# Two softmax attentions and a squared-ReLU layer: transposes moved from VectorE and TensorE to the DMA engines

## The chip, the core and the metric

The kernel runs on one core of a Trainium2 chip. The engines are TensorE (PE in the profile, its weight loads PEld), VectorE (DVE), ScalarE (ACT), GpSimd (POOL) and SyncE (SP, which only issues DMAs). The metric is the device time of one launch in microseconds; less is better.

## What is computed

Eight batches, eight heads, a sequence of 576 rows, head size 64. 32 packed queries `p` per head first attend over the whole sequence, and then every row of the sequence attends over the 32 packed results, which serve as keys and as values. The output, with heads side by side (4608 rows of 512), goes through two layers with a squared ReLU between them.

```python
def sm_attn(qq, kk, vv):
    s = scale * np.matmul(qq, kk.transpose(0, 1, 3, 2))
    s = s - np.max(s, axis=-1, keepdims=True)
    a = np.exp(s)
    a = a / (np.sum(a, axis=-1, keepdims=True) + 1e-09)
    return np.matmul(a, vv)
p_packed = sm_attn(p, k, v)
out = sm_attn(q, p_packed, p_packed)
...
h = x @ w_in                    # 512 -> 2048
g = np.maximum(h, 0.0) ** 2
return (g @ w_out)              # 2048 -> 512, float32
```

## The kernel before

The order of all work is written out by hand, as some 1,390 words in one string, `ORDER`; each word is one step, and each engine runs its steps in the order of the words. There is no loop over batches in the program: steps of different batches are woven together, the layers of batch b between the attention of batch b + 1.

A word names a step, a batch and a quad (four heads, so that two quads make a batch): `kT30` is the turn of the keys of batch 3, quad 0. The steps of the attention, in the order of its data:

- `Lk`, `Lq`, `Lv`: loads of keys, queries and values, issued by POOL, which casts them from float32 to bfloat16 on the way (lines 233 to 242). Keys and queries come as 128 partitions (4 heads x 32 rows) by 18 x 64. Each of the three kinds has three buffers, so a load waits for the reader of the third load before it.
- `kT`, `qT` (lines 279, 285): DVE transposes keys and queries in 32 x 32 blocks of pairs of bfloat16. The result has 32 pairs of head elements on 32 partitions per head. Two buffers each.
- `s1` (line 295): scores of the packed queries. A contraction over 64 head elements is done in two passes (`e`, even and odd elements) of 32 rows, on 32x32 tiles of the PE array. From batch 2 on both quads of a batch go together, eight tiles side by side; for the second quad, `group` (line 245) moves heads to other tile positions.
- `m1` (DVE maximum, line 316), `x1` (ACT exponential with its sum, line 321), `rd` (reciprocal, line 328).
- `eT` (line 339): six PE transposes of the exponentials into PSUM; `eo` copies them to SBUF on DVE or ACT (lines 334, 332).
- `pv` (line 352): the packed result, contracted over the sequence in six chunks; `pp` scales it (lines 360, 362), `bd` is a DVE transpose of it for the second scores (line 367); `pt`, `po` are a PE transpose and its copy (lines 372, 332, 334), which `w0` and `w1` read.
- `s2` (line 295), `t2`, `m2`, `sb`, `x2`, `su`, `a2`, `aT`: scores of the sequence rows and the second softmax, mostly on DVE (lines 383 to 415).
- `w0`, `w1` (line 422): the packed results times `w_in`, on 64x32 tiles; `W0`, `W1` copy this to SBUF.

Then `h` (line 438, first layer), `r` (ReLU on ACT or DVE, lines 444, 446), `q` (square on DVE, line 479), `o` (second layer, line 490), and `c` (copy to SBUF and two stores from SP's queue, line 510).

The packed queries of batches 0 and 1 are loaded first by SP (line 170) and turned by DVE; those of batches 2 to 7 come by one POOL DMA (`Pr`, line 552), and `Pt` turns and scales them on DVE (lines 211, 217).

PSUM: the tag `a` (two buffers of two banks) is shared by all scores, transposes, `ps_pv` and `ps_wp`; `ps_h` and `ps_o` have two buffers each in the later stages. `o_sb` has three buffers.

Of the kernel before, what the change touches and what calls it, by code (L numbers as in the profile page):

```python
# [21 lines left out]
D = 64  # L22
# [9 lines left out]
PAIRED = range(2, 8)  # L32
# [9 lines left out]
Lk00 Lk01 Lq00 kT00 P0 Z32 s100 kT01 I m100 x100 Z5 s101 m101 x101 Lq01 P1 Z7 eT00 Lv00 eo00:a Lk10 Z10 pv00 rd00  # L42
qT00 rd01 qT01 pp00:v bd00 eT01 kT10 Lv01 Z3 s200 Wi00 Wi01 pt00 eo01:a Lk11 Z5 pv01 s110 pp01:a t200 pt01 Wi10 bd01
m200 sb00:p m110 s201 x110 t201 x200 m201 su00 Z10 eT10 po01:v eo10:a a200:v Z12 w001 sb01:p po00:a x201 su01 Wi11
aT00 w000 Lv11 a201:p kT11 W001:a Z11 s111 Lv10 W000:a aT01 h0.8 m111 h0.11 r0.8:a h0.9 r0.11:v h0.2 x111 r0.9:a
w101 q0.8 h0.3 r0.2:v W101:a Lq11 eT11 eo11:a rd11 h0.10 Lq10 q0.9 rd10 w100 r0.3:v W100:a h0.1 r0.10:v h0.0 q0.3
pv11 Wo0 r0.1:a q0.11 Pr r0.0:v h0.5 q0.2 pp11:a h0.6 pv10 r0.5:a qT11 r0.6:a pt11 bd11 q0.1 h0.14 pp10:a q0.10
r0.14:a h0.12 s211 h0.15 q0.0 r0.12:a h0.7 r0.15:a po11:v qT10 r0.7:a w011 Wo2 t211 Lk21 h0.13 q0.6 W011:a q0.5 h0.4
bd10 r0.4:a w111 s210 r0.13:v Wo1 o0.0 q0.7 m211 sb11:v o2.0 x211 W111:a t210 o2.1 Lk20 m210 o3.0 Wo3 o1.0 o0.1 o0.2
q0.15 o1.1 su11 o1.2 Pt pt10 po10:a q0.4 o2.2 o3.1 w010 Lv20 w110 o0.3 Lq21 o3.2 o3.3 o0.4 q0.13 o2.3 W010:a Lv21  # L50
o1.3 kT21 q0.12 W110:a kT20 a211:p o1.4 q0.14 sb10:p x210 su10 o1.5 o0.5 s12 o2.4 o2.5 a210:p m120 x120 o0.6 m121
o1.6 aT11 aT10 o0.7 c0:v o1.7 x121 o2.6 c1:a o2.7 h1.0.0 qT21 h1.0.6 eT20 eT21 rd21 r1.0.6:v rd20 r1.0.0:a o3.4
h1.0.4 Lq20 eo20:a h1.0.2 pv20 eo21:v pv21 r1.0.2:v r1.0.4:a h1.0.1 pp20:v h1.0.5 pt20 pp21:v c2:a r1.0.1:a r1.0.5:a
o3.5 po20:a bd21 h1.0.12 h1.0.3 w020 q1.0.2 o3.6 r1.0.12:a r1.0.3:a h1.0.7 h1.0.13 q1.0.0 Lk30 qT20 o3.7 W020:a bd20
o4.0 r1.0.13:a c3:a r1.0.7:v q1.0.1 h1.0.10 q1.0.6 h1.0.11 q1.0.3 s22 r1.0.10:a h1.0.8 r1.0.11:a r1.0.8:a h1.0.9
Lq30 o4.1 t220 h1.0.14 r1.0.9:a o4.2 t221 q1.0.4 r1.0.14:a h1.1.0 r1.1.0:a pt21 h1.0.15 m221 o4.3 po21:a h1.1.2
r1.0.15:a w021 w120 q1.0.5 h1.1.10 o5.0 sb21:v r1.1.2:a W021:a o4.4 h1.1.8 m220 x221 Lv31 r1.1.10:a sb20:v o5.1 Lk31
r1.1.8:a x220 o4.5 h1.1.3 r1.1.3:a h1.1.11 o4.6 r1.1.11:a kT30 W120:a h1.1.4 kT31 r1.1.4:a w121 q1.0.7 h1.1.1 o5.2
o4.7 r1.1.1:a h1.1.6 o5.3 su20 W121:a su21 Lq40 h1.1.5 r1.1.5:a r1.1.6:v c4:a o5.4 s13 a221:v h1.1.7 q1.1.0 r1.1.7:a
h1.1.14 q1.1.5 o5.5 r1.1.14:a h1.1.15 r1.1.15:a a220:v Lk40 o5.6 aT21 o5.7 q1.1.1 q1.1.2 h1.1.12 q1.1.3 Lk41 aT20  # L60
c5:a h1.1.13 Lq31 r1.1.12:a o6.0 o6.1 h1.1.9 r1.1.13:a r1.1.9:a o6.2 Lv41 m131 h2.0.2 q1.1.4 r2.0.2:a h2.0.3 o6.3
m130 h2.0.0 r2.0.3:a o6.4 h2.0.4 kT40 q1.1.7 r2.0.0:a x130 o7.0 h2.0.8 r2.0.4:a o6.5 Lv30 r2.0.8:a eT30 x131 h2.0.6
rd30 o7.1 eo30:v h2.0.7 o7.2 eT31 r2.0.6:a q1.1.6 o6.6 o6.7 qT30 r2.0.7:a rd31 qT31 q2.0.1 h2.0.1 h2.0.14 pv30
eo31:a r2.0.1:a pv31 o7.3 pp31:a c6:a r2.0.14:v h2.0.5 q2.0.0 o7.4 h2.0.10 pp30:a r2.0.5:v o7.5 bd30 r2.0.10:a
h2.0.12 pt30 r2.0.12:a o7.6 h2.0.9 h2.0.11 po30:a kT41 w030 bd31 w130 r2.0.11:a W030:a r2.0.9:v q2.0.3 h2.1.6 q2.0.2
r2.1.6:a h2.0.13 o7.7 r2.0.13:a o8.0 W130:v c7:a h2.0.15 h2.1.7 r2.0.15:a s23 q2.0.4 h2.1.0 r2.1.7:v q2.0.7 o8.1
r2.1.0:a h2.1.14 t230 o8.2 t231 h2.1.12 r2.1.14:a Lq41 q2.0.6 m231 o8.3 o8.4 Lv40 r2.1.12:a pt31 q2.0.5 h2.1.1 o8.5
o9.0 h2.1.15 r2.1.1:a h2.1.4 r2.1.4:a o8.6 r2.1.15:a o9.1 o8.7 m230 h2.1.10 po31:v sb31:v o9.2 h2.1.13 x231 o9.3
o9.4 r2.1.10:a sb30:v su31 r2.1.13:a h2.1.8 q2.1.3 c8:a w131 w031 q2.1.0 h2.1.11 o9.5 x230 r2.1.8:v r2.1.11:a a231:v
W031:a q2.1.6 h2.1.2 o9.6 r2.1.2:v h2.1.5 su30 o9.7 a230:v q2.1.7 h2.1.3 aT31 W131:a r2.1.5:a o10.0 o10.1 o10.2 s14  # L70
h2.1.9 aT30 c9:a r2.1.3:a o10.3 q2.1.1 h3.0.8 o10.4 o10.5 r2.1.9:a r3.0.8:a h3.0.2 h3.0.0 m140 q2.1.4 x140 m141
r3.0.2:a x141 q2.1.2 q2.1.5 o11.0 eT40 eo40:v h3.0.6 o11.1 r3.0.0:a rd41 o11.2 h3.0.3 eT41 r3.0.6:a h3.0.1 qT40 qT41
r3.0.3:a o10.6 Lk50 eo41:a r3.0.1:v h3.0.7 o10.7 rd40 q3.0.1 pv40 pv41 r3.0.7:a pp40:v q3.0.0 h3.0.4 h3.0.5 pt40
o11.3 r3.0.4:a h3.0.9 c10:v Lk51 o11.4 r3.0.5:v r3.0.9:a q3.0.4 o11.5 h3.0.10 o11.6 po40:a pp41:a h3.0.12 pt41 bd40
r3.0.10:a q3.0.3 h3.0.14 r3.0.14:v r3.0.12:a o11.7 h3.0.15 bd41 w140 po41:a q3.0.2 w040 r3.0.15:v h3.1.2 W040:a
o12.0 W140:a o12.1 r3.1.2:v h3.0.11 o12.2 o12.3 kT51 q3.0.7 r3.0.11:v h3.1.0 kT50 s24 h3.1.4 r3.1.0:v c11:a o12.4
t241 o12.5 r3.1.4:a o12.6 h3.1.5 o12.7 r3.1.5:a h3.0.13 q3.0.5 r3.0.13:a o13.0 h3.1.6 o13.1 m241 c12:a sb41:v h3.1.3
r3.1.6:a r3.1.3:a x241 t240 o13.2 h3.1.1 r3.1.1:a o13.3 h3.1.7 o13.4 o13.5 r3.1.7:a q3.0.6 Lv51 m240 sb40:v h3.1.8
Lq51 w141 w041 q3.1.2 o13.6 o14.0 r3.1.8:a x240 h3.1.9 su41 o13.7 o14.1 Lv50 h3.1.14 W041:a c13:a a241:v r3.1.9:v
r3.1.14:a h3.1.15 o14.2 su40 W141:a o14.3 q3.1.1 h3.1.12 o14.4 r3.1.15:a s15 aT41 h3.1.10 o14.5 Lv61 a240:v o14.6  # L80
r3.1.12:a q3.1.0 h3.1.13 r3.1.10:a aT40 q3.1.4 m150 m151 h4.0.2 r3.1.13:a o15.0 o15.1 h4.0.10 r4.0.2:a o14.7 q3.1.6
q3.1.3 o15.2 x150 h4.0.4 r4.0.10:a o15.3 h3.1.11 c14:v r4.0.4:v x151 eT50 eo50:a q3.1.7 eT51 h4.0.8 r3.1.11:v q3.1.5
o15.4 h4.0.5 Lk61 r4.0.8:v o15.5 eo51:v h4.0.12 Lk60 r4.0.5:v pv50 pv51 h4.0.9 rd51 r4.0.12:a o16.0 h4.0.11 Lq50
r4.0.9:a q4.0.4 rd50 o16.1 r4.0.11:a pp50:v pp51:a h4.0.3 o16.2 pt51 qT50 o15.6 h4.0.0 po51:v r4.0.3:a r4.0.0:a
q4.0.5 o15.7 Lq60 h4.0.14 pt50 c15:a q4.0.1 h4.0.1 o16.3 r4.0.14:a o16.4 po50:v r4.0.1:v h4.0.15 h4.1.0 w050 q4.0.2
w150 bd51 r4.1.0:a r4.0.15:a o16.5 h4.0.6 kT60 q4.0.0 h4.1.1 r4.1.1:a q4.0.7 o16.6 bd50 r4.0.6:v o17.0 h4.1.2 Lk71
W050:a h4.1.3 r4.1.2:a W150:v o17.1 o17.2 qT51 r4.1.3:a h4.0.13 kT61 r4.0.13:a h4.0.7 q4.0.6 s25 h4.1.6 t251
r4.0.7:a t250 o16.7 q4.1.0 o17.3 o17.4 o17.5 c16:a m250 r4.1.6:a h4.1.10 h4.1.4 r4.1.4:a o17.6 sb50:v w151 w051
r4.1.10:a h4.1.5 h4.1.11 o17.7 m251 o18.0 r4.1.5:a h4.1.8 r4.1.11:a o18.1 Lq71 q4.0.3 qT60 c17:a h4.1.9 Lk70 o18.2
q4.1.2 o18.3 o18.4 o18.5 r4.1.8:a sb51:v W051:a o18.6 o19.0 x250 r4.1.9:a x251 W151:a h4.1.12 h4.1.7 q4.1.1 o18.7  # L90
c18:a o19.1 r4.1.12:a Lq61 su50 s16 a250:v o19.2 su51 a251:v m160 h4.1.14 r4.1.7:a o19.3 h4.1.13 o19.4 aT50
r4.1.14:a x160 o19.5 aT51 q4.1.3 m161 Lv60 h4.1.15 o19.6 r4.1.13:a h5.0.10 o20.0 r4.1.15:a h5.0.2 x161 q4.1.5 q4.1.4
o19.7 r5.0.2:a o20.1 eT61 r5.0.10:v h5.0.6 h5.0.3 eT60 c19:v r5.0.6:a o20.2 r5.0.3:v eo60:a q4.1.6 h5.0.4 eo61:v
r5.0.4:a h5.0.7 o20.3 q5.0.1 rd61 pv60 r5.0.7:a rd60 pp60:v pv61 h5.0.0 q4.1.7 Lv70 h5.0.11 o20.4 pt60 r5.0.0:a
h5.0.1 o20.5 r5.0.11:v pp61:a h5.0.5 o21.0 r5.0.1:a o20.6 po60:a h5.0.8 r5.0.5:a h5.1.2 qT61 kT71 q5.0.5 w160 q5.0.3
bd60 w060 q5.0.2 r5.0.8:a r5.1.2:a W060:a o21.1 h5.0.9 kT70 o21.2 W160:a r5.0.9:v bd61 Lv71 o20.7 o21.3 h5.1.3
q5.0.0 r5.1.3:v h5.0.14 s26 t260 h5.0.15 c20:a r5.0.14:a h5.0.12 r5.0.15:a r5.0.12:a o21.4 h5.1.0 o21.5 r5.1.0:a
q5.1.1 t261 h5.1.12 r5.1.12:a h5.1.1 o22.0 q5.0.4 r5.1.1:a h5.0.13 m260 o22.1 r5.0.13:v o21.6 h5.1.4 pt61 r5.1.4:a
sb60:v po61:a h5.1.13 o21.7 r5.1.13:a h5.1.6 o22.2 m261 q5.0.7 h5.1.14 x260 r5.1.6:a o22.3 r5.1.14:a o22.4 c21:a
sb61:v h5.1.5 h5.1.7 r5.1.5:a r5.1.7:a o22.5 su60 w061 q5.1.6 w161 q5.0.6 h5.1.15 h5.1.8 Lq70 x261 a260:v r5.1.15:a  # L100
q5.1.0 q5.1.2 aT60 o22.6 W061:a o22.7 o23.0 h5.1.10 r5.1.10:v o23.1 o23.2 r5.1.8:a h5.1.11 o23.3 c22:a o23.4 W161:a
su61 h5.1.9 q5.1.3 s17 o23.5 r5.1.11:a o24.0 a261:v aT61 o23.6 m170 h6.0.6 m171 r5.1.9:a o24.1 h6.0.2 o23.7 x170
# [525 lines left out]
```

## Time and profile before

| | |
|---|---|
| Time, median of 2 runs | 250.86 us (250.03 and 251.68) |
| Span of the profiled execution | 248.6 us |
| Median less span | 2.3 us |
| PE, DVE, ACT, POOL busy | 95%, 78%, 59%, 18% |
| Granted clock of PE | 0.99 of full speed over the span |
| DMA by POOL (loads) | 18.55 MB, 47.1% of 16 DMA engines' span |
| DMA by SP (stores) | 9.44 MB, 15.0% |

The page gives no device time for the profiled execution apart from its span, so the difference of 2.3 us stands for what lies around the span.

How to read it: a row of the page's groups names the line, the engine, the operation and the tiles (out<-in), how often it ran, its busy time, the mean of one in ns, and the idle time of its engine just before with what ended it. Matmuls overlap, so the mean of one (379 ns for 512 columns) is longer than the pitch at which they follow each other. In the timeline, each line is a run of like instructions with its start and its length, both in microseconds. "To landing" is the time from the issue of a DMA to its last byte.

### The profile page before, as it was taken

How to read it: one execution, taken by the hardware profiler on the slowest of the kernel's cores; microseconds unless marked ns; L12 is line 12 of the kernel's file. 1: busy time of each engine (PE TensorE's matmuls, PEld its weight loads, DVE VectorE, ACT ScalarE, POOL GpSimd, SP SyncE). 2: the span in 40 equal slices, each digit the busy share in tenths (PEclk: the TensorE clock that was granted, in tenths of full speed). 3: DMA queues.
4: the chain of work that ended last, by engine and by line, in shares of the span. 5: the costliest groups of instructions: out<-in, count | busy, mean ns of one | idle time of the engine just before them, and what ended most of it. 6: DMA issues, size and time to landing. Idle time of an engine off the chain costs nothing.

```text
span 248.6 us, 6041 instructions
## 1 busy us (share of the span) xinstructions
PE 237.1 (95%) x2415; PEld 132.2 (53%) x2447; DVE 194.2 (78%) x411; ACT 145.7 (59%) x316; POOL 45.8 (18%) x75
## 2 busy tenths in 40 slices
PE   8998899998999999999999999999999999999992
PEld 5655554465556554655456555655555555555540
DVE  1888899978988899979887998898897798644710
ACT  2346784476968748755764658676957555353100
POOL 8329634350401500033000230010000000000000
PEclk9999999999999999999999999999999999999997
DMA  6999999999791992269812794252121213211323
GB/s 112 203 207 205 206 197 209 197 142 259 161 171 64 157 211 45 46 93 187 185 42 45 135 130 122 64 90 56 42 45 42 45 42 82 49 42 44 70 63 82
DMA packets 23358, 28.52 MB, mean 115 GB/s; under 512 B 4257, under 2 KB 14753, under 8 KB 23329
## 3 DMA queue, kind: packets, MB, share of 16 engines
q0 software_dynamic: 16880, 18.55, 47.1%
q1 hardware_dynamic: 6288, 9.44, 15.0%
q8 instruction: 19, 0.31, 0.5%
q10 hardware_dynamic: 160, 0.13, 0.2%
q14 instruction: 11, 0.08, 0.1%
HBM read 37.22 MB, written 9.44 MB: 188 GB/s over the span
## 4 chain that ended last, share of the span: by engine, by line
PE 81%; DMA 10%; issue 2%; DVE 2%; POOL 2%; ACT 1%; SPq 0%; ACTq 0%; POOLq 0%
PE ps_o L490 48%; PE ps_h L438 24%; DMA v_b<-in_v_dram 4%; PE ps_wp L422 3%; PE ps_s L295 3%; DMA w_in_bf<-in_moe_w_in_dram 3%; DMA out_dram<-o_sb 3%; PE ps_e1T L339 1%; PE ps_pv L352 1%; POOL k_b L242 1%; DVE mx L387 1%; POOL d L391 0%; ACT r L444 0%; POOL q_b L242 0%; PE ps_ppT L372 0%
## 5 line engine op out<-in xcount | busy, mean ns | idle before, releaser
L490 PE MATMUL ps_o<-w_out_bf,gT 128*128 128x512 bf16 x544 | 144.2, 379 | 2.0 <-issue 0.5
L444 ACT ACTIVATE r<-ps_h 128x288 bf16<-128x288 f32 (+1 forms) x181 | 73.1, 426 | 55.9 <-PE ps_h L438 47.5
L438 PE MATMUL ps_h<-a2T,wp 128*128 128x288 bf16 x512 | 91.9, 286 | 1.4 <-ACT r L444 1.4
L490 PEld LDWEIGHTS <-gT 128*128 128x128 bf16 x576 | 54.9, 98 | 42.1 <-issue 3.3
L438 PEld LDWEIGHTS <-wp 128*128 128x128 bf16 x512 | 47.4, 98 | 44.4 <-issue 7.7
L479 DVE TENSOR_TENSOR gT<-r 128x576 bf16<-128x576 bf16 x128 | 54.7, 448 | 5.2 <-ACT r L444 4.9
L446 DVE TENSOR_SCALAR r<-ps_h 128x288 bf16<-128x288 f32 (+1 forms) x59 | 28.5, 484 | 20.0 <-PE ps_h L438 18.8
L332 ACT CAST wp<-ps_wp 128x1024 bf16<-128x1024 f32 x29 | 28.9, 1016 | 3.8 <-PE ps_wp L422 3.7
L332 ACT COPY o_sb<-ps_o 128x512 f32<-128x512 f32 x27 | 15.9, 588 | 10.8 <-PE ps_o L490 9.4
L321 ACT ACTIVATE e<-ps_s,nm 128x576 bf16<-128x576 f32 x16 | 11.8, 736 | 13.0 <-DVE nm L316 13.0
L233 POOL DMA_DIRECT2D v_b<-in_v_dram x16 | 11.1, 695 | 44.2 <-PE ps_pv L352 22.5
L279 DVE STREAM_TRANSPOSE kT<-k_b 128x576 uint32<-128x576 uint32 x16 | 15.0, 943 | 5.1 <-DMA k_b<-in_k_dram 5.1
L263 PE MATMUL ps_idle<-nought 128*128 128x288 bf16 x95 | 14.4, 304 | 1.1 <-DVE nought L178 1.1
L383 DVE STREAM_TRANSPOSE s<-ps_s 128x576 f32<-128x576 f32 x16 | 12.0, 767 | 2.4 <-PE ps_s L295 2.4
L401 DVE TENSOR_REDUCE sums<-e 128x18 f32<-128x576 f32 x16 | 11.9, 741 | 1.4 <-ACT e L396 1.3
L242 POOL DMA_DIRECT2D k_b<-in_k_dram x16 | 9.0, 562 | 21.4 <-DVE kT L279 12.5
L422 PE MATMUL ps_wp<-w_in_bf,ppT 64*32 64x512 bf16 x256 | 11.4, 382 | 0.8 <-DMA w_in_bf<-in_moe_w_in_dram 0.7
L316 DVE TENSOR_REDUCE nm<-ps_s 128x1 f32<-128x576 f32 x16 | 11.6, 739 | 0.6 <-PE ps_s L295 0.6
L285 DVE STREAM_TRANSPOSE qT<-q_b 128x576 uint32<-128x576 uint32 x16 | 12.0, 761 | 0.0
L387 DVE TENSOR_REDUCE mx<-s 128x18 f32<-128x576 f32 x16 | 11.9, 743 | 0.1
L396 ACT ACTIVATE e<-d 128x576 f32<-128x576 f32 x16 | 11.0, 685 | 1.6 <-DVE d L391 1.4
L263 PEld LDWEIGHTS <-nought 128*128 128x128 bf16 x95 | 9.2, 103 | 4.9 <-issue 1.2
(47 smaller groups left out, 153.0 us busy)
## 6 DMA issues: line engine op xcount, KB each, us to landing
out_dram<-o_sb SPq DMA_DIRECT2D x70, 128.0 KB, 2.8
k_b<-in_k_dram POOLq DMA_DIRECT2D x16, 288.0 KB, 8.1
v_b<-in_v_dram POOLq DMA_DIRECT2D x16, 288.0 KB, 7.4
q_b<-in_q_dram POOLq DMA_DIRECT2D x10, 288.0 KB, 7.2
w_in_bf<-in_moe_w_in_dram POOLq DMA_DIRECT2D x4, 512.0 KB, 12.5
w_out_bf<-in_moe_w_out_dram POOLq DMA_DIRECT2D x4, 512.0 KB, 13.8
q_b<-in_q_dram POOLq DMA_DIRECT2D x12, 144.0 KB, 3.9
p_b<-in_p_dram POOLq DMA_DIRECT2D x1, 192.0 KB, 11.5
```

What stands on the lines that cost most here:

```text
L263: self.nc.tensor.matmul(ps[:, :HALF], lhsT=self.nought[:, :P], rhs=self.nought, start=True, stop=True)
L279: return self.nc.vector.transpose(t["kT"][:].rearrange("p (j l a) e -> p a j l e", j=J, a=3).bitcast(U32).rearrange("p a j l e -> p a j (l ...
L285: return self.nc.vector.transpose(t["qT"][:].rearrange("p s e -> p (s e)").bitcast(U32), t["q"][:].rearrange("p t d -> p (t d)").bitcast(U32))
L332: engine.copy(out, x)
L383: nc.vector.transpose(s2[:].rearrange("p (a t) i -> p a (t i)", a=2), t["ps_s2"][:, :, :HALF])
L387: self.nc.vector.tensor_reduce(out=t["mx"], in_=t["s2"], op=ALU.max, axis=AX.X)
L422: self.nc.tensor.matmul(ps[NP * h:NP * h + NP, c, :], lhsT=t["ppT"][D * c:D * c + D, NP * g:NP * g + NP], rhs=self.w_in_bf[D * c:D * c + D ...
L438: self.nc.tensor.matmul(ps, lhsT=t["wp"][:, fb // n, fb % n * P:(fb % n + 1) * P], rhs=t["a2T"][:, hf * HALF:(hf + 1) * HALF], start=(qd = ...
L444: engine.activation(r, ps, ACT.Relu)
L446: engine.tensor_scalar_max(r, ps, 0.0)
L479: (engine or self.nc.vector).tensor_tensor(out=out, in0=r, in1=r, op=ALU.mult)
L490: self.nc.tensor.matmul(self.o[tt], lhsT=self.gT[:, fb, a:a + P], rhs=self.w_out_bf[:, fb, :], start=(i == 0), stop=(i == self.NFB - 1))
```

## The change

From batch 2 on (`TURNED`):

- Keys and queries (`kT`, `qT`) are transposed by DMA from SP's queue, 128 x 1152 into nine blocks of 128 x 128: rows of even `t` come to partitions 0 to 63 and of odd `t` to 64 to 127, with the 64 head elements on the partitions.
- The packed queries are loaded twice, side by side (`p_d`, two POOL DMAs), scaled by DVE and turned by one DMA (`pX`).
- Scores contract over 64 rows in one pass, on 64x32 tiles (`scores2`): 16 matmuls a batch and step where there were 32. The second scores read `ppT`, the PE transpose of the packed result, and `bd` goes; `t2` undoes the new order of rows.
- The exponentials are written into one of two fixed tiles with chunks padded to 128 columns, and a DMA from SP's queue turns them (`eT`); the PE transposes and the copies `eo` go.
- `group` goes; each query load is one DMA.

The words of `ORDER` are the same 1,390. Moved are `kT` and `qT` (each to just behind its load, or behind the scores that free its buffer, so mostly earlier), and `pt` with `po` (to just behind `pp`).

```diff
@@ p_rest
-        g0, g1 = 2 * self.NQ, self.B * self.NQ
-        self.p_turn(g0, g1)
-        x = self.pT[:, g0:, :]
-        self.nc.vector.tensor_scalar_mul(x, x, SCALE)
+        self.nc.vector.tensor_scalar_mul(self.p_d, self.p_d, SCALE)
+        self.nc.sync.dma_start_transpose(self.pX, self.p_d[:].rearrange("p g e d -> p (g e d)"))
@@ new
+    def st_turned(self, t, n):
+        x = t[n + "T"] = self.tp.tile([P, 2 * S], BF16, name=n + "T")[:].rearrange("p (t l) -> p t l", l=P)
+        self.nc.sync.dma_start_transpose(x, t[n][:].rearrange("p t d -> p (t d)"))
+    def scores2(self, *quads):
+        for h in range(QH):
+            c = slice(NP * h, NP * h + NP)
+            for e in range(2):
+                r = slice(D * e, D * e + D)
+                for ps, x, y in quads:
+                    self.nc.tensor.matmul(ps[c, e, :HALF], lhsT=x[r, c], rhs=y(r, c), start=True, stop=True)
@@ st_s1
+                x.append((t["ps_s1"], self.pX[:, (b - TURNED[0]) * self.NQ + qd, :],
+                          lambda r, c, y=t["kT"]: y[r, :, c].rearrange("p (a b) l -> p b l a", a=3)))
+            return self.scores2(*x)
@@ st_s2
+                x.append((t["ps_s2"], t["ppT"], lambda r, c, y=t["qT"]: y[r, :, c]))
+            return self.scores2(*x)
@@ st_exp1
+            e1 = t["e1"] = self.e1s[(b * self.NQ + qd) % len(self.e1s)]
+            t["den"] = self.sm.tile([P, 1], F32, name="den")
+            self.nc.scalar.activation(e1[:, :, :PS].rearrange("p (a b) s -> p a b s", a=2),
+                                      t["ps_s1"][:, :, :HALF].rearrange("p a (b s) -> p a b s", b=3), ACT.Exp,
+                                      bias=t["nm"], accum_out=t["den"])
@@ st_e1T
+            t["e1T"] = self.tp.tile([P, J, P], BF16, name="e1T")
+            self.nc.sync.dma_start_transpose(t["e1T"], t["e1"][:].rearrange("p j s -> p (j s)"))
+            return
@@ step, word "Pr"
-            self.nc.gpsimd.dma_start(self.p_b[:, g0:g1, :], self.packed(g0, g1))
+            for e in range(2):
+                self.nc.gpsimd.dma_start(self.p_d[:, :, e, :], self.packed(TURNED[0] * self.NQ, self.B * self.NQ))
@@ ORDER, batch 2
-... h1.0.0 qT21 h1.0.6 eT20 eT21 rd21 ... Lq20 eo20:a h1.0.2 pv20 eo21:v pv21 ... h1.0.1 pp20:v h1.0.5 pt20 pp21:v c2:a
+... h1.0.0 h1.0.6 eT20 eT21 rd21 ... Lq20 qT20 eo20:a h1.0.2 pv20 eo21:v pv21 ... h1.0.1 pp20:v pt20 po20:a h1.0.5 pp21:v pt21 po21:a c2:a
...
```

## The prediction

> **What bounds the kernel now.** I read the page's busy shares first, then the busy time by stretches, then the timeline around the steps that change, then the landing times of the DMAs. (Columns of the stretches: length, busy us of PE, PEld, DVE, ACT and POOL with their instructions, granted clock, DMA share, GB/s.)
>
> ```profile
> span 248.6 us, 6041 instructions
> PE 237.1 (95%) x2415; PEld 132.2 (53%) x2447; DVE 194.2 (78%) x411; ACT 145.7 (59%) x316; POOL 45.8 (18%) x75
> ```
> ```profile
> 47.00:100.00 53.00, 51.56 (x593) 28.92 (x602) 45.88 (x98) 38.41 (x88) 12.55 (x21) 1.00 0.81 152
> 100.00:150.00 50.00, 49.48 (x526) 27.70 (x532) 44.26 (x95) 31.92 (x74) 8.08 (x14) 1.00 0.62 112
> 150.00:209.00 59.00, 58.42 (x602) 32.42 (x610) 50.46 (x109) 39.60 (x92) 1.23 (x2) 1.00 0.28 58
> ```
>
> From the first scores of batch 2 (46.9 us) on, PE is busy 97 to 99% of every stretch at a granted clock of 1.00. The starts of its runs follow each other at the pitch of the matmuls (216 ns for 512 columns, 123 for 288); the few larger gaps of some 220 ns fall where a 512-column record is missing. So PE has no waits to give away: work taken from PE shortens the end one for one, and each new wait of PE lengthens it one for one. DVE, at 86 to 89%, does not end PE's waits. What decides is whether a DMA put into PE's chain lands before PE gets there.
>
> **What the change takes from PE.** The timeline shows the price of each removed step, from its start to the next run's.
>
> ```profile
> 46.91 0.70 PE L295 MATMUL ps_s<-kT,pT 32*32 32x288 bf16 x32
> 47.55 0.82 PE L490 MATMUL ps_o<-w_out_bf,gT 128*128 128x512 bf16 x3
> ...
> 102.46 0.50 PE L339 MATMUL ps_e1T<-ident,e 128*96 128x128 bf16 x6
> 102.80 0.41 PE L438 MATMUL ps_h<-a2T,wp 128*128 128x288 bf16 x2
> ...
> 110.51 0.62 PE L422 MATMUL ps_wp<-w_in_bf,ppT 64*32 64x512 bf16 x16
> 111.07 0.42 PE L438 MATMUL ps_h<-a2T,wp 128*128 128x288 bf16 x2
> ```
>
> Six transposes of the first softmax cost 0.34 us of PE; 12 such groups (batches 2 to 7, two quads) go: -4.0 us. The 32 score matmuls of a batch cost 0.64 us in four rounds of eight tiles. The new 16 stand on the 64x32 tiles that ps_wp uses; its 16 take 0.56 us, two rounds of 512 columns at 0.216 and 0.125 beside them. Two rounds of 288 are then 0.125 + 2 x 0.123 = 0.37 us, 0.27 less in each of 12 score steps: -3.2. Keys are now read with a step of three blocks per column, which no row shows; if that undid the gain, it would be 0. PE: -7.2 (at least -4.0).
>
> DVE loses 12 kT (943 ns), 12 qT (761), 12 bd (195) and its copies of e1T, some 25 us, and ACT its e1T copies (794 ns each). Neither ends anything while PE is the bound: counted as nothing.
>
> **What it adds: 37 turns on SP's queue.** 24 are of 288 KB (keys, queries), 12 of 192 KB (the exponentials, two per batch) and one of 384 KB (packed queries). SP had one load and the output stores; now the stores, the turns and the waits for loads stand in one line. No turn is in this trace. The nearest rows are SP's own DMAs.
>
> ```profile
> out_dram<-o_sb SPq DMA_DIRECT2D x70, 128.0 KB, 2.8
> k_b<-in_k_dram POOLq DMA_DIRECT2D x16, 288.0 KB, 8.1
> p_f<-in_p_dram SPq DMA_DIRECT2D x1, 128.0 KB, 2.2
> ```
> Landing of the output stores issued from 50 to 56 us, while loads were in flight:
> ```profile
> DMA to landing us min/median/max: 6.9/7.3/7.6
> ```
> And of those issued after 150 us, with few loads beside them:
> ```profile
> DMA to landing us min/median/max: 2.3/2.4/3.5
> ```
>
> Even 128 KB takes 2.2 to 2.4 us with the DMAs idle and over 7 behind loads. In the packet records, p_f's 512 packets of 256 bytes took 18 ns each, 0.6 us on 16 engines, so 1.6 of its 2.2 us is fixed. A turn moves rows of 128 two-byte elements, 256 bytes. At p_f's pace the exponentials (768 rows) take 0.86 us, keys 1.3, packed queries 1.7: the lower bound. If every element went by itself, the 4-byte packets (9 ns) would give 9216 x 9 = 83 us for keys: the upper bound. The row is nearer, but a block that is crossed is no plain copy; I take twice p_f's pace: 1.7, 2.6 and 3.5 us, and 3.3 us from issue to landing of one idle turn of exponentials.
>
> [...]
>
> Now each place where PE can wait for a turn.
>
> (a) *First scores of batch 2.* The last k_b before them landed at 44.66; DVE turned it from 45.63 to 46.57, PE began at 46.91. The second copy of the packed queries delays this load by 0.6 (in the trace p_b landed 0.64 after w_out ahead of it). SP then issues kT20 (0.6 of SP per issue, as the stores) and behind it, at 45.9, the turn of the packed queries, with loads in flight until 51.4. Landing as a store there, 7.3, plus 3.0 more transfer, would be 56; since some loads drain meanwhile I take 55.1, a wait of 8.2. With p_f's pace and nothing ahead it is 2.5; behind all loads, 12.
>
> (b) *Exponentials of batch 2.* From the scores' end to pv are 5.6 us (47.61 to 53.21), less 0.7 for the transposes gone: 4.9. The second exp ends 2.4 after the scores; a turn among loads lands 7.3 + 1.2 later: 10.9. Wait 6.0 (1 to 10).
>
> (c) *Batches 3 to 7.* The timeline of batch 4 shows the slack:
> ```profile
> 101.81 0.20 ACT L321 ACTIVATION_READ_ACCUMULATOR e<-ps_s,nm 128x1 f32 x1
> ...
> 102.91 0.20 ACT L321 ACTIVATION_READ_ACCUMULATOR e<-ps_s,nm 128x1 f32 x1
> ...
> 105.93 0.56 PE L352 MATMUL ps_pv<-v_b,e1T 96*32 96x64 bf16 x48
> ```
> The second exp ends at 103.11, pv begins at 105.93: 2.8. The others: 78.08 to 80.59, 130.05 to 132.81, 157.73 to 161.22, 184.23 to 186.80; less 0.67 each the five sum to 10.8. No load was in flight there. With exps 1.1 apart the second turn lands 1.6 + 2 x 1.7 - 1.1 = 3.9 after its exp; 0.5 for issue and release makes 4.4. Waits: 5 x 4.4 - 10.8 = 11.2. At p_f's pace it is 3.0 each, 4.3 in all.
>
> (d) *The turn of the packed result* (pt) moves to just behind pv, since the new scores read ppT. Before, pp ended at 54.04 and pt began at 54.20 with four layer-1 matmuls between it and pv; now one or two (0.245) stand where pp (0.35) and two releases (0.2) must pass. 12 x 0.3 = 3.5 (1 to 5).
>
> (e) *Queues behind.* On SP the exponentials of batch 3 stand behind qT31, which waits for a load that POOL issues behind one that waits for kT30. Before, that query landed at 71.84, 4.8 us before the first exp ended; one loaded turn in that line uses this up. The late ones also bunch ACT's and DVE's work behind PE's waits. I add 4 (0 to 10). Stores are hidden by three o_sb buffers: 72 issues in 249 us; held longer than two tiles' time (7 us), the copy and PE's ps_o would wait.
>
> **Sum.** -7.2 + 8.2 + 6.0 + 11.2 + 3.5 + 4.0 = +25.7 us on the span of 248.6: 274.3. The median of the runs is 250.86, 2.3 above that span, so I forecast 277. All lower bounds: +1.6, 252.5. All upper ones, with the exponentials of rival 1: +66, 317.
>
> **Rivals.** *1: a turn holds SP or the DMAs for 4 us or more.* For it: no row shows a turn, and the bound by elements is far. Then a pair of exponentials lands 1.6 + 8 - 1.1 + 0.3 = 8.8 after the second exp: 5 x 8.8 - 10.8 = 33; (a) 12, (b) 10, (d) 3.5, and 24 keys and queries on a 96 us occupied queue cost some 15 in (e): 250.9 - 7.2 + 73.5 = 317, from there upwards. Against: p_f's 256-byte packets. [...]
>
> *2: the queues are harmless and only batch 2 waits*, all at p_f's pace: 252 to 256. Against: 7.3 us for stores among loads.
>
> *3, the other side: the turns hide.* If one landed within 1.9 us of its exp and the packed queries before 46.9, only (d) at 1 and 1 us of (a) stay: 250.9 - 7.2 + 2 = 245.7. It decides from 2 us landing; the fastest idle DMA of SP took over 2.0, and loads triple that.
>
> *4: the 64x32 tiles don't run side by side* in this order: 16 x 0.123 = 2.0 instead of 0.37, 12 x 1.6 = 19 more, 296. Against: ps_wp.
>
> **Numbers.** The forecast (258 to 300) 0.52; rival 1 to 340 0.20, beyond 0.08; rival 4 0.06; rival 2 0.09; rival 3 0.05. The range 254 to 340 leaves out some 0.18. About 2% (5 us) is what a measurement can tell. Faster comes from rival 3's lower part, 0.04; within 2% (to 255.9) from the rest of it and rival 2, 0.07; slower 0.89.
>
> **What would show it.** Right: PE near 88% with idle time before pv and the first scores of batch 2, ended by the turns' DMAs; e1T landing 3 to 5 us after issue, keys of batch 2 over 6; 16 score matmuls in 0.37 us; DVE near 170 us busy. Wrong: landings under 2.5 us (then 255), turns of 4 us on SP (then 317), or PE waits at the relu or at loads instead.

## The result and the profile after

The changed kernel took 294.01 us (median of 2 runs, 293.16 and 294.86), the kernel before 250.86. The ratio is 1.171, with a 95% interval of 1.158 to 1.184: 43 us slower. The forecast was 277 with a range of 254 to 340. Times and ratios are those of each kernel's undisturbed executions; where a profile below is of a longer one, its span is given beside it.

The page of the kernel after, with the lines that answer to those shown of before:

```profile
span 291.4 us, 5579 instructions
...
PE 245.8 (84%) x2183; PEld 128.2 (44%) x2183; DVE 173.1 (59%) x367; ACT 142.5 (49%) x311; POOL 44.4 (15%) x72
...
PEclk9999999557789899999999979999999799999999
...
PE 61%; DMA 25%; SPq 3%; DVE 3%; ACT 2%; POOL 2%; issue 1%; ACTq 0%; POOLq 0%
```

PE's share fell from 95 to 84%; its busy time rose from 237.1 to 245.8 us, though it has 232 matmul records fewer; in part that is because some ran at half the clock (19.4 us of the busy time). The chain that ended last now runs through DMAs for a quarter of its length, and the granted clock drops to half in slices 8 and 9. The same line of the kernel before:

```profile
PE 81%; DMA 10%; issue 2%; DVE 2%; POOL 2%; ACT 1%; SPq 0%; ACTq 0%; POOLq 0%
```

PE's waits after (engine, tile and line, releaser: us in total, times, longest):

```profile
PE ps_s L299 <- DMA pX<-p_d: 18.1, 1, 18.1
PE ps_pv L382 <- DMA e1T<-e1x: 13.1, 8, 3.6
PE ps_s L299 <- DMA kT<-k_b: 4.3, 1, 4.3
PE ps_h L472 <- ACT r L478: 1.6, 5, 0.4
```

35.5 us of waits end with one of SP's turns, half of them in one place. By stretches (columns: length, busy time of PE, PEld, DVE, ACT and POOL with their instructions, granted clock, DMA share, GB/s):

```profile
47.00:100.00 53.00, 26.02 (x232) 12.21 (x232) 17.82 (x38) 17.13 (x38) 7.75 (x13) 0.77 0.96 156
100.00:150.00 50.00, 48.38 (x451) 25.23 (x437) 32.58 (x71) 30.41 (x73) 6.50 (x11) 0.97 0.88 152
150.00:209.00 59.00, 53.25 (x486) 27.09 (x485) 38.16 (x84) 33.97 (x79) 4.69 (x8) 0.97 0.80 142
```

In 53 us around batch 2's first scores PE worked 26, where it had worked 51.6. The timeline of the three longest waits, each in the brackets at the end of its line:

```profile
65.16 0.80 PE L299 MATMUL ps_s<-kT,pX 64*32 64x288 bf16 x16 [18.05 <-DMA pX<-p_d]
...
76.14 0.51 PE L382 MATMUL ps_pv<-v_b,e1T 96*32 96x64 bf16 x24 [3.56 <-DMA e1T<-e1x]
...
99.66 0.79 PE L299 MATMUL ps_s<-kT,pX 64*32 64x288 bf16 x15 [4.27 <-DMA kT<-k_b]
```

What the turns share the DMA engines with, in 14 us of the first wait, 47 to 61 (queue: packets, MB, share of 16 engines; q0 has POOL's loads, q1 SP's turns):

```profile
q0 software_dynamic: 1850, 2.26, 93.4%
q1 hardware_dynamic: 1863, 0.47, 26.5%
```

Both queues moved nearly the same number of packets (1850 and 1863; from 46 to 51 us, 784 and 785), but a load's packet has 1.2 KB on average and a turn's 256 bytes: SP's queue got 0.47 of 2.73 MB. This is where the theory for the experiments comes from: from the equal counts I estimate that the two queues take turns, one packet of each at a time. A packet of this trace is mostly one piece of 256 to 2304 bytes.

### The profile page after: what moved, and what is told of

It reads as the page before. It is cut to its first block, busy times and chain, and to the rows that moved or that the text cites. A ratio compares the mean times of both kernels' runs of the same rounds, so it can differ in the third digit from the quotient of the medians.

```text
span 291.4 us, 5579 instructions
## 1 busy us (share of the span) xinstructions
PE 245.8 (84%) x2183; PEld 128.2 (44%) x2183; DVE 173.1 (59%) x367; ACT 142.5 (49%) x311; POOL 44.4 (15%) x72
## 4 chain that ended last, share of the span: by engine, by line
PE 61%; DMA 25%; SPq 3%; DVE 3%; ACT 2%; POOL 2%; issue 1%; ACTq 0%; POOLq 0%
PE ps_o L524 37%; PE ps_h L472 18%; DMA e1T<-e1x 6%; DMA k_b<-in_k_dram 5%; DMA pX<-p_d 5%; DMA kT<-k_b 4%; DMA v_b<-in_v_dram 3%; DMA q_b<-in_q_dram 3%; PE ps_s L299 2%; PE ps_wp L456 2%; SPq L268 2%; PE ps_pv L382 1%; ACT r L478 1%; SPq L364 1%; SPq L544 1%
## 5 line engine op out<-in xcount | busy, mean ns | idle before, releaser
L524 PE MATMUL ps_o<-w_out_bf,gT 128*128 128x512 bf16 x576 | 154.6, 389 | 0.1
L472 PE MATMUL ps_h<-a2T,wp 128*128 128x288 bf16 x512 | 94.6, 293 | 1.6 <-ACT r L478 1.6
L524 PEld LDWEIGHTS <-gT 128*128 128x128 bf16 x576 | 56.3, 100 | 46.2 <-issue 6.7
L472 PEld LDWEIGHTS <-wp 128*128 128x128 bf16 x512 | 48.6, 100 | 49.0 <-issue 13.2
L513 DVE TENSOR_TENSOR gT<-r 128x576 bf16<-128x576 bf16 x128 | 55.9, 461 | 22.2 <-ACT r L478 22.0
L299 PE MATMUL ps_s<-kT,pX 64*32 64x288 bf16 x96 | 5.2, 450 | 22.3 <-DMA pX<-p_d 18.1
L340 ACT ACTIVATE e1x<-ps_s,nm 128x576 bf16<-128x576 f32 x12 | 8.8, 736 | 22.5 <-DVE nm L334 22.5
L382 PE MATMUL ps_pv<-v_b,e1T 96*32 96x64 bf16 x384 | 6.1, 201 | 13.2 <-DMA e1T<-e1x 13.1
L435 DVE TENSOR_REDUCE sums<-e 128x18 f32<-128x576 f32 x16 | 11.9, 745 | 2.6 <-ACT e L430 2.4
L240 POOL DMA_DIRECT2D q_b<-in_q_dram x16 | 8.8, 548 | 28.7 <-DMA qT<-q_b 15.7
L299 PEld LDWEIGHTS <-pX 64*32 64x32 bf16 x96 | 1.1, 93 | 25.1 <-DMA pX<-p_d 18.5
L421 DVE TENSOR_REDUCE mx<-s 128x18 f32<-128x576 f32 x16 | 11.9, 744 | 0.1
```

The lines of the kernel that those rows point to most:

```text
L240: self.nc.gpsimd.dma_start(x, s)
L299: self.nc.tensor.matmul(ps[c, e, :HALF], lhsT=x[r, c], rhs=y(r, c), start=True, stop=True)
L421: self.nc.vector.tensor_reduce(out=t["mx"], in_=t["s2"], op=ALU.max, axis=AX.X)
L435: nc.vector.reduce_sum(out=sums, in_=t["e2"], axis=AX.X)
L472: self.nc.tensor.matmul(ps, lhsT=t["wp"][:, fb // n, fb % n * P:(fb % n + 1) * P], rhs=t["a2T"][:, hf * HALF:(hf + 1) * HALF], start=(qd = ...
L513: (engine or self.nc.vector).tensor_tensor(out=out, in0=r, in1=r, op=ALU.mult)
```

## The experiments

**Theory:** a turn of 288 KB is 72 short packets on each DMA engine, and each lets one long packet of the loads by; beside loads it lands after 10 us and more. **Rivals:** the transposing itself or its issue is slow; the turns clog SP's queue for what stands behind them; the clock, lost in the waits, is what costs.

### The turn by itself

```diff
+ y = tile([P, 9, P]);      sync.dma_start_transpose(y, src)          # turn
+ y = tile([P, 9, P + 2]);  sync.dma_start(y[:, :, :P], src)          # pieces of 256 bytes
+ y = tile([P, 9, P]);      sync.dma_start(y, src)                    # whole, 2304 bytes
```

> Not the layers at all: the output is only filled with zeros; SyncE's DMAs are measured one by one. Three kinds of 288 KB moves from SBUF to SBUF: the transposing DMA, a plain copy in 256-byte pieces, a plain copy in 2304-byte pieces; first each alone, twice, then each issued behind the first landing of 14 key loads (2304-byte packets) on GpSimd's queue, and the transposing one beside 14 value loads (768-byte packets). Alone: about 3.3 us to landing for the transposing one, 2.5 to 3.5 for the copies. Theory (queues alternate packet by packet on each DMA engine, so 72 short packets per engine wait for 72 long ones): beside key loads the transposing DMA and the 256-byte copy both take 12 to 17 us, the 2304-byte copy (8 packets per engine) 4 to 7; beside value loads the transposing one 6 to 9. Rival (the transposing itself is slowed, by its unit or its issue): the 256-byte copy lands as the 2304-byte one, in 4 to 7, and the transposing one alone takes 12 or more. Rival (moves share the engines by bytes): all three copies 4 to 7.

Landing times from issue, in one execution, each of these measured once: first the turn alone; then beside key loads the turn, the copy in 256-byte pieces and the copy in whole rows; last the turn beside value loads.

```profile
DMA to landing us min/median/max: 3.2/3.2/3.2
...
DMA to landing us min/median/max: 18.1/18.1/18.1
...
DMA to landing us min/median/max: 18.4/18.4/18.4
...
DMA to landing us min/median/max: 7.6/7.6/7.6
...
DMA to landing us min/median/max: 12.1/12.1/12.1
```

Alone, the copies landed in 3.0 to 3.1 and 2.4 us. Beside the same loads the plain copy in 256-byte pieces is as late as the turn, and the same bytes in 2304-byte rows land in less than half the time. So it is the size of the packets, not the transposing; the theory holds, though all four landings lie 0.6 to 3.1 us above its numbers. The packet records show what it left out: beside loads the first packet moved 4.1 to 4.5 us after the issue, against 1.2 to 1.3 alone, and no run shows why. From the first packet to the last it then took 13.3, 13.6, 2.5 and 7.1 us. For the first two, 72 load packets of 192 ns are 13.8 us; for the last, 72 of 78 ns are 5.6. The transposing DMA was about as fast as the copy in equal pieces, alone (3.2 us against 3.0 to 3.1) and beside loads (18.1 against 18.4), and slower than the copy in whole rows (2.4 and 7.6).

### The exponentials back on TensorE

```diff
- if b in TURNED: ... self.nc.sync.dma_start_transpose(t["e1T"], ...); return
+ for j in range(J): self.nc.tensor.transpose(ps[:, j, :], t["e1"][:, j, :PS], self.ident)
```

> The changed kernel, but the exponentials of batches 2 to 7 are transposed by TensorE again (six transposes and a copy), so that only keys, queries and packed queries are turned by DMA. Theory (turns land late because their 256-byte packets alternate with the loads' long packets, and PE then waits and loses half its clock): the waits of pv for e1T, 4.6 us in batch 2 and 8.9 in batches 3 to 7, and the half clock behind them (some 3) go, 12 x 0.34 = 4.0 us of PE comes back: 294 - 13.5 - 3 + 4 = 281 us (277 to 285). The 18.2 us wait for pX and that for kT of batch 3 stay. Rival (the turns clog SP's queue, so that the ones behind are late): with 12 turns fewer ahead of them kT of batch 3 lands earlier too and its 4.6 us go as well: below 276. Rival (PE's waits are only renamed, the loads end last): 290 or more.

282.5 us, ratio 1.124 (1.117 to 1.131); the theory said 281. The waits for e1T are gone. That for pX stays (19.9), and so does that for kT of batch 3 (5.6 for 4.3), although the turns of exponentials ahead of it on SP are gone: they were not what made it late.

### Batch 2 back on VectorE and TensorE

```diff
- TURNED = range(2, 8)
+ PAIRED = range(2, 3)
+ TURNED = range(3, 8)          # kT2x qT2x pt2x po2x at their old words, heads of batch 2 paired as before
```

> Batch 2 goes back to VectorE and TensorE (keys, queries, packed queries, exponentials; steps at their old places, both quads side by side), batches 3 to 7 stay turned by DMA. Theory: the 18.2 us wait for pX, the 4.6 us for e1T of batch 2 and the half clock behind both (some 5) go, 0.8 us of PE work comes back: 294 - 28 + 1 = 267 us (263 to 271). pX itself still lands 10 us or more after its issue, but nobody waits. Rival (the loads that the turns hold back are what is late, whoever reads first): the wait comes back at the first scores of batch 3 with 8 us or more, 275 to 285.

277.4 us, ratio 1.101 (1.095 to 1.107): 10 us above the theory, inside the rival's range, but for another reason. The first wait did go; others grew. pX, which nobody waits for now, still landed 14.2 us after its issue. The stores issued from 51.57 us stood behind it in SP's queue and landed after 9.7 to 10.5 us, where such stores took 6.9 to 7.6 in the kernel before. This came through to PE:

```profile
62.84 0.59 ACT L370 COPY o_sb<-ps_o 128x512 f32<-128x512 f32 x1 [3.85 <-DMA out_dram<-o_sb]
...
63.79 0.71 PE L485 MATMUL ps_h<-a2T,wp 128*128 128x288 bf16 x4 [3.26 <-ACT r L491]
```

ScalarE's copy waits for one of three o_sb buffers to be stored, the ReLU stands behind the copy, and PE's `h` behind the ReLU: 3.3 us. Beside it come 1.5 us more of waits for e1T in batches 3 to 7 (4.0 in batch 5, whose turn landed in 4.8 us beside a load), 0.7 for kT of batch 5, and some 6.0 us lost to half clock where I had left 2.6: 8.9 of the 10.4. My reading, which no run tests by itself, is that without the long wait ahead of them batches 3 to 7 meet their loads at other places.

### The keys read as they lie

```diff
- lambda r, c: y[r, :, c].rearrange("p (a b) l -> p b l a", a=3)
+ lambda r, c: y[r, :, c]
...
- t["ps_s1"][:, :, :HALF].rearrange("p a (b s) -> p a b s", b=3)
+ t["ps_s1"][:, :, :HALF].rearrange("p e (a b l) -> p e b l a", a=3, b=3)   # the exponential's input
```

> The turned keys are read by the score matmuls in the order in which they lie (32 neighbours at a time instead of single columns 768 bytes apart); the exponential puts the columns in order as it reads PSUM. Theory (the column step halves the rate of the moving operand): the score matmul falls from 450 to about 290 ns, the step of 16 from 0.72 to 0.39 us; 6 x 0.33 = 2.0 us less if PE isn't waiting there, so 292 (291 to 294). Rival (two 64-row tiles with different lhsT cost this): no change, 450 ns stays. The exponential may take longer than 736 ns; at up to 900 this costs under 1 us.

292.4 us from two executions, ratio 1.163 (1.154 to 1.172), against 1.158 to 1.184 for the changed kernel: where the theory has it, but inconclusive in time. The groups show the mechanism. First the changed kernel's two kinds of score matmul, then this one's first kind (profile of a 295.2 us span); the mean of one is behind the bar:

```profile
L299 PE MATMUL ps_s<-kT,pX 64*32 64x288 bf16 x96 | 5.2, 450 | 22.3 <-DMA pX<-p_d 18.1 <-DMA kT<-k_b 4.3
L299 PE MATMUL ps_s<-qT,ppT 64*32 64x288 bf16 x96 | 2.8, 288 | 0.0
```
```profile
L299 PE MATMUL ps_s<-kT,pX 64*32 64x288 bf16 x96 | 3.3, 312 | 22.2 <-DMA pX<-p_d 18.1 <-DMA kT<-k_b 4.1
```

In the timeline of batch 5 the step of 16 goes from 0.72 us (157.65 to 158.37) to 0.40 (158.28 to 158.68). The exponential takes 738 ns where it took 736. So the columns 768 bytes apart cost 0.32 us a step; the time of the whole is ended by DMAs, and it doesn't show there. Why that step slows the matmul, no run shows.

### TensorE kept awake in its waits

```diff
+ def fill(self, n):      # words F140 ahead of s12, F28 pv20, F36 s13, F13 pv50, F21 pv60, F18 pv71
+     ps = self.turn32("ps_fill")
+     for _ in range(n): self.nc.tensor.matmul(ps[:, 0, :HALF], lhsT=self.nought[:, :P], rhs=self.nought, ...)
```

> The changed kernel with TensorE kept busy where it waited: 140 matmuls on zeros ahead of the first scores of batch 2, 28 ahead of pv20, 36 ahead of the first scores of batch 3, 13, 21 and 18 ahead of pv50, pv60 and pv71, some 0.123 us each, into a PSUM tile that nobody reads. The waits stay as long as before. Theory (each idle time of 2.8 us or more is followed by a stretch at half the clock, 7.6 us lost in all): the granted clock stays at 1.00 through those places and the time falls by 5 to 7.6 us, to 287 to 290. Rival (the clock falls for another reason, such as load on the chip): the half-clock stretches stay and the time is 294 to 297.

296.2 us, ratio 1.175 (1.167 to 1.184): no gain, though the clock did what the theory says, but for one stretch of 3.4 us:

```profile
PEclk9999999997999999999999999999999999999999
```

pX landed 4.5 us later in this execution, which could have hidden a gain. So once more without the 140:

> As the kernel with matmuls on zeros in TensorE's waits, but without the 140 ahead of batch 2's first scores; the 28, 36, 13, 21 and 18 ahead of pv20, batch 3's first scores, pv50, pv60 and pv71 stay. In the run with all of them pX landed 4.5 us later than in the changed kernel, which hid what the clock gave. Theory (half clock behind the later waits costs 5 us or so that nothing else covers): 294 - 3 to 5 = 289 to 291. Rival (a faster TensorE only reaches the next late DMA earlier, so that its waits grow by what the clock gives): 293 to 296, with longer waits for e1T and kT than 4.6, 4.6, 2.8, 2.8 and 2.4 us, the filled part counted in.

298.4 us, ratio 1.182 (1.176 to 1.187): no gain either, and above both ranges. Its profile (a 304.7 us span, so the waits of one long execution) has the rival's picture: the five filled waits, with 0.1225 us for each matmul of the fill, were 4.4, 6.3, 3.6, 4.3 and 3.6 us, against 4.6, 4.6, 2.8, 2.8 and 2.4. But there too pX was late, by 6.2 us, with no fill ahead of it: its landing took 13.9 us in the changed kernel, and 13.9, 15.4, 17.6 and 18.8 in the four others that issue the same work up to it. And the clock was only partly kept: it stood at half for 30.7 us, in which PE was busy for 12.3, against 34.1 and 19.4 in the changed kernel; 23.9 of them began in the first wait, which had no fill. That the clock falls to half behind long waits is shown: in the changed kernel behind five of the six places where PE waited 2.4 us or more, and with all of them filled for 3.4 us alone. Whether this costs anything of its own stays open, and so does what the fill does to the DMAs.

### The exponentials alone

```diff
+ TURNED = range(3, 8)          # into the kernel before: st_exp1, st_e1T, eo and pv of the change, nothing else
```

> The kernel before with one part of the change alone: the exponentials of batches 3 to 7 are turned by DMA, at the unchanged places in the order; keys, queries and batch 2 stay on VectorE. SP's queue carries only these ten turns and the stores. Theory (an idle turn lands 2.8 us after its issue, the second one 1.24 later at the earliest, against 2.1 to 2.8 us of slack): TensorE gives up 5 x 0.67 = 3.4 us and waits 0.6 to 1.6 us per batch, 3 to 8 in all, with half-clock stretches only behind the longest: 252.5 us (249.5 to 256). Rival (the turns behind other turns on SP made the waits): waits under 2 us in all, 249 or less.

265.3 us, ratio 1.053 (1.046 to 1.059): some 13 us above the theory and 9 above its range, and the rival fell further. In its profile (a 265.1 us span) the waits for e1T are 11.9 us where I had at most 8, and some 4.4 us were lost at half clock, 1.7 of them behind a wait for the ReLU at 60.8 us; the longest, 4.7, is for the second turn of batch 3, which was issued at 81.18, as a query load was at 81.14, and landed after 6.7 us. The other nine landed in 2.7 to 3.2 us and still made 1.0 to 2.5 us of waits in each of batches 4 to 7: an idle turn alone is too slow for this slack.

### The same with pv later

```diff
- x140 ... x141 ... eT40 ... eT41 ... pv40 pv41 ...
+ x140 eT40 ... x141 eT41 ... (some 2 us of h and o) ... pv40 ... pv41
```

> As the one above, but each turn is issued right behind its exponential and pv of batches 3 to 7 stands some 2.0 us of TensorE's other work later (the steps behind it only as far as they must). Theory: the waits for e1T vanish, the 3.4 us stay: 250.9 - 3.4 = 247.5 us (246.5 to 249). Rival (what is moved makes new waits at pp, pt or the second scores, as everything behind pv is closer together): 250 to 253.

256.7 us, ratio 1.014 (1.007 to 1.021). The order alone took 9 us off: the waits for e1T fell from 11.9 to 1.9. It is not the 247.5 of the theory, since 1.9 stayed and the waits at the ReLU grew from 1.4 (in the kernel before) to 4.4, a wait such as the rival means; but the time is above the rival's 250 to 253 too.

### And the queries

```diff
+ "qT": lambda: self.st_turned(t, "q") if b in TURNED else self.st_q(t)      # and st_s2 by scores2
```

> As the one above, and the queries of batches 3 to 7 are turned by DMA too (each at VectorE's old place or just behind the turns of the exponentials of its batch, ahead of the second scores by 3 us or more), with the second scores in one pass over 64 rows. Theory: 5 x 0.24 = 1.2 us of TensorE less, landing 3.3 us when no load is in flight: 246.3 us (245 to 249). Rival (a turn among loads holds SP for 2 to 7 us; stores or the exponentials behind it are late): 249 to 256, with waits of ACT for the stores or of TensorE for e1T or qT.

252.3 us, ratio 1.003 (0.999 to 1.007). PE's list of waits has none for e1T or qT any more. The timeline shows what is:

```profile
59.99 0.59 ACT L361 COPY o_sb<-ps_o 128x512 f32<-128x512 f32 x1 [2.31 <-DMA out_dram<-o_sb]
60.47 0.72 ACT L481 ACTIVATE r<-ps_h 128x288 bf16<-128x288 f32 x2
...
60.94 0.71 PE L475 MATMUL ps_h<-a2T,wp 128*128 128x288 bf16 x4 [1.73 <-ACT r L481]
```

It is the chain of batch 2's experiment; the kernel before has it too, with 0.85 us of PE at 59.55. The other waits behind ScalarE, 0.7 us and less each, stand where the moved steps had come close together.

### A fourth buffer, and ScalarE relieved

```diff
- self.op = pool("op", 3)
+ self.op = pool("op", 4)                   # and pp41:v po40:v po60:v po61:v c23:v
```

> As the kernel with exponentials and queries by DMA (252.3 us), with two causes of its new waits at the ReLU taken away: a fourth buffer for o_sb (a copy on ScalarE stood 2.3 us for a store that landed late among loads, and TensorE 1.87 us behind it), and five small copies of batches 4, 6 and 7 (pp41, po40, po60, po61 and one output copy) on VectorE instead of ScalarE. Theory (its 4.6 us of removed TensorE work were eaten by 4.7 us of waits behind ScalarE, not by the turns): 1.9 + 1.5 us come back, 249 us (248 to 250.5). Rival (the gain is eaten by DMA landings): no change, 252.

249.4 us, ratio 0.9905 (0.9875 to 0.9934), as expected; PE's waits at the ReLU are 0.7 us for 4.0. How much of this is the buffer's, the kernel before with that edit alone tells:

> The kernel before with nothing but a fourth buffer for o_sb. Theory: its one wait of 1.0 us at the ReLU near 58 us (ScalarE's copy waits for a store that lands 7 us after its issue among loads) goes: 1.0 us less than the kernel before, 250.7 if that runs at 251.7. This separates what the fourth buffer gives from what the turns give in the runs beside it.

249.8 us, ratio 0.9935 (0.9910 to 0.9959). The intervals overlap: with exponentials and queries turned by DMA, and five copies off ScalarE, there is no gain beyond the buffer's that could be measured.

### And the keys from batch 4

```diff
+ KEYS = range(4, 8)            # keys by st_turned at VectorE's old words, read as they lie
+ p_d for KEYS; "Px": scaled and turned behind qT31
```

> As the one above, and the keys of batches 4 to 7 are turned by DMA as well, at VectorE's old places, read by the scores in the order in which they lie; their packed queries are loaded twice and turned behind the queries of batch 3. Theory: 4 x 0.24 = 1.0 us of TensorE less, as the keys have 10 us or more until their scores: 248 us (247 to 250). Rival (key turns issued among loads hold SP for up to 5 us and land after 10 or more, so that stores or exponentials behind them are late): 250 to 256, with waits for e1T or o_sb.

247.5 us, ratio 0.984 (0.981 to 0.988): 4.0 us less than the kernel before it was measured beside (251.5), and clear of the fourth buffer alone, by 2.3 us. The 4.0 us are 1.6% of the time, under the 2% that the prediction took for what a measurement can tell, but the interval leaves out 1. No run has the buffer and the five copies without any turn, so what the turns gave of the 2.3 is not separated. This is the fastest version of all. Its page, and the landing times of its key turns:

```profile
span 246.1 us, 5658 instructions
...
PE 234.0 (95%) x2211; PEld 127.0 (52%) x2243; DVE 178.9 (73%) x383; ACT 141.1 (57%) x307; POOL 45.1 (18%) x74
```
```profile
DMA to landing us min/median/max: 6.0/8.6/12.8
```

The turns of keys are as late among loads as ever. But their scores come 10 us or more behind their issue, and PE is busy 95% of a shorter span.

## Why the prediction was right, and where it was off

The direction, its cause (a DMA in PE's chain that lands after PE gets there) and the range were right; the sum was 17 us short: +25.7 on the span foretold, +42.8 measured. Waits below are those of the views, so that they can be looked up.

- **PE's work, -7.2:** -5.0. The transposes gave their 4.0. The second scores took 0.39 us a step for 0.37 foretold, -0.24 x 6. The first scores got slower, 0.72 for 0.63, +0.08 x 6, as the columns read 768 bytes apart take 450 ns for 288. I had named this as the unknown ("with a step of three blocks per column, which no row shows") and put the gain's loss at 0 at worst; it was below that.
- **(a) First scores of batch 2, +8.2 (2.5 to 12):** 18.1. This is the step that failed: "Landing as a store there, 7.3, plus 3.0 more transfer". A store has 2 KB packets, a turn 256-byte ones, and beside loads it is the count of packets that sets the time (the same 288 KB landed after 18.4 us in 256-byte pieces, after 7.6 in whole rows). The row to take was the load's packet: in the records of the trace a key load's 2304 bytes hold an engine for 192 ns, 72 of those are 13.8 us, and kT and pX landed after 12.2, 18.0 and 13.9, the last two with turns ahead of them. "Behind all loads, 12" was no upper bound either: the words "with loads in flight until 51.4" misread the trace of before, where seven more loads are issued from 49.06 to 52.42 us and land until 66.17. And "0.6 of SP per issue, as the stores" was the stores' row, not a turn's. The issues of the second key turn and of pX on SP (ns, then the start in us):

```profile
L268 SPq DMA_TRANSPOSE kT<-k_b x1: 5323/5323/5323, 45.8 to 45.8; - x1
...
L220 SPq DMA_TRANSPOSE pX<-p_d x1: 9477/9477/9477, 51.2 to 51.2; - x1
```

The second key turn was issued at 45.77 and its issue held SP for 5.3 us, so that pX was issued at 51.19 and not at 45.9. Yet that key turn, which the scores need too, itself landed only at 63.8, 1.3 us ahead of pX: the landing decided, not the hold.
- **(b) Exponentials of batch 2, +6.0:** 4.4, for another reason. I had a turn among loads; the loads had drained during the wait of (a), and both landed in 2.8.
- **(c) Batches 3 to 7, +11.2:** 8.8. The idle turn landed in 2.8 us for 3.3 foretold, and SP issued the second 1.3 to 1.4 behind the first, not 1.7. In batch 6 they stood behind three turns of keys and queries on SP, which my sum put under (e). "No load was in flight there" was not quite so: in the kernel before two query loads are issued at 79.56 and 80.09, in batch 3's place, and beside such loads the exponentials alone had their longest wait.
- **(d) The packed result's turn, +3.5:** 0.7. PE waited for pp 0.5 us in batch 6 and 0.2 in batch 7; the views show no such wait in the others, where I had 0.3 in each of twelve.
- **(e) Queues behind, +4.0:** 4.3 at the first scores of batch 3 for a key turn that landed after 10.9, and 1.6 behind the ReLU, where the kernel before had 1.4.
- **Not foreseen:** some 7.6 us lost where PE ran matmuls at half its clock, an estimate from how much farther apart they start there (427 ns for 216 with 512 columns, 240 for 123 with 288). The stretches are 52.0 to 69.1, 75.9 to 82.7 and three of 3.4 us, all lengths multiples of 3.4; the two at 168.0 and 229.5 stand behind waits of only 2.5 and 2.4 us.

All these are 39.1 of the 42.8, if the 7.6 are counted as additive, which no run shows; 3.7 stay without an account. The sum came as near as it did because (b), (c) and (d) were 6.8 us too high together.

**Rival 1** (a turn holds SP or the DMAs for 4 us or more) was half true: an idle turn held SP for 1.21 to 1.37 us, but the second key turn, among loads, for 5.3, and pX behind two others for 9.5. Its price for the exponentials, 33 us, did not come, because theirs ran without loads. **Rivals 2 and 3** fell with the 18.1. **Rival 4** fell with the 0.39 us step. Of the signs named, DVE's 170 us (173.1), keys of batch 2 over 6 (12.2 and 18.0) and idle time ahead of pv and batch 2's scores came; PE was 84% for 88, and e1T at 2.8 lay under its 3 to 5.

## What to carry to other kernels

Cost a DMA that runs beside others by its packets, not by its bytes: the turn's 72 on each engine, each put behind a load's packet of 192 ns, make 13.8 us by my estimate; measured were 13.3, and 4.1 to 4.5 us before the first of them. The turns here had 256-byte packets and lost most against long rows: 18.1 us beside packets of 2304 bytes, 12.1 beside packets of 768. Taking work off a full engine paid here only where its DMA was issued early enough: the same turns cost 43 us where PE came to them at once, and with the crowded batches left alone, the keys read as they lie and pv 2 us later they gained 2 beyond what a fourth store buffer gave by itself, together with five copies moved off ScalarE. Look past the engine that was relieved: each gain here first reappeared as a wait of ScalarE, for a store that landed late or for copies packed closer together.

## What the hardware showed that I had not expected

- A 288 KB DMA of 256-byte pieces, transposing or not, landed 3.0 to 3.2 us after its issue alone and 18 beside loads with 2304-byte packets; the turn took 12.1 beside 768-byte ones.
- A turn's issue occupied SP longer when others were in flight: with the turn by itself it took 1.3 us idle and 2.3 to 3.1 beside loads, in the changed kernel 9.5 with two turns ahead of it, and up to 13.0 in a variant. A plain copy in 256-byte pieces took 0.6 to 0.7 us of SP, idle or beside loads.
- In the run of the turn by itself, a DMA of SP beside loads moved its first packet 4.1 to 4.5 us after the issue, transposing or not; alone after 1.2 to 1.3.
- A wait of 1.9 us (the kernel with pv later, at 60.9) was followed by 3.4 us at half the clock; one of 2.6 us in the changed kernel was not.
- The same turn of the packed queries took 13.9 to 18.8 us in kernels that are alike up to it.
- A matmul whose moving columns lie 768 bytes apart took 450 ns; one of the same shape on the turned queries, 288.
